# Spectral mixer and squared-ReLU layer on one core: butterfly outputs of three frequency pairs from TensorE, with a reordered first stage

## The chip, the cores and the metric

The kernel runs on 1 core of one Trainium2 chip. The metric is the device time of one execution in microseconds (us). Three runs of the kernel before gave 182.49, 182.58 and 182.77 us, with a median of 182.58 us.

Engine names in the text: PE is TensorE, DVE is VectorE, ACT is ScalarE, POOL is GpSimd, SP is SyncE, which issues most DMAs here. "L333" is line 333 of the kernel before.

## The reference

```python
x = A_x                                   # (1, 2048, 512) bf16
n = layernorm(x)                          # over the last axis
X = rfft2(n) * (w_r + 1j * w_i)           # w: (2048, 257)
h = x + irfft2(X).astype(bfloat16)
t = layernorm(h) @ w1 + b1                # w1: (512, 1792)
h2 = h + (relu(t) ** 2 @ w2 + b2)         # w2: (1792, 512)
```

The two-dimensional transform over 2048 x 512 points is computed as a chain of matrix products with sine and cosine tables that the kernel makes itself.

## The kernel before, in words

The work has three phases, one after the other.

**First phase (statistics and stage 1).** The 2048 rows lie as 16 groups `g` of 128 rows in `xs`. Each group needs a mean and a variance (`mv1`), a reciprocal root (`rs1`), and the table `KF` scaled by it, `KFr[:, g]`, which is called a fold. Means and variances come from DVE (`ln1_stats`, L205 and L208) for 13 groups and from two passes on ACT (`ln1_sums`, L197) for groups 3, 7 and 11. `ln1_rstd` (L211, L212) runs on POOL, `ln1_fold` (L216) on DVE. `stage1(g0)` multiplies groups g0 and g0+1 on PE (L231, L233) and evacuates the result from PSUM into `Bt` with one ACT copy (L241), or, with `split=True`, half on ACT and half on DVE (L238). Beside this, POOL makes the angles of the table GF (`angles_g`, L179), ACT takes their sine (L113), POOL builds the identity `ident`, and POOL issues two gathers (`w_reversed`, L145) that load rows of the weights w in reversed order into `WB`, rows 16 to 22. The spectral step of every pair but the first reads one of these rows.

**Second phase (spectral).** The 16 values of the frequency index k1 are handled as 8 pairs `pr`. For each pair:
- `stage2(pr)`: 8 matmuls of 256 columns (L326), then one ACT copy into `U` (L333); for pair 0 the copy is split (L331).
- `stage3(pr)`: for pairs 1 to 7, 4 matmuls of 512 columns (L351 to L354) give two sums A and B, then one ACT copy puts them into `AB` (L356). Pair 0 is its own case (L343 to L347) and writes `X` directly.
- `butterfly(pr)`: on DVE, A plus swapped B and A minus swapped B give `X` (L365, L366), two instructions.
- `spectral(pr)`: on DVE, two products with the weights (`mA`, `mB`, L375), two instructions into `Z` (L380, L381), two into `M` (L388, L390). The two butterfly instructions of the next pair are placed inside: one before the `Z` pair and one before the `M` pair.
- `stage4(pr)`: 8 matmuls (L405, L406), then one ACT copy into `T` (L413), for the last pair split over ACT and DVE (L410, L411).

The loop over `pr` (L426) issues in each turn `stage3(pr+2)`, `stage2(pr+3)`, `stage4(pr-1)`, `spectral(pr)`. So the ACT queue in a turn reads: copy AB(pr+2), copy U(pr+3), copy T(pr-1). In the turn `pr == 4` the sine of the table GI (L113) follows on ACT behind T(3) and so stands ahead of AB(7). The copies of the transposed tables, `KI` (L418) and `EI` (L258), stand between the other ACT copies. POOL has little to do here: it casts `b1f` (L446).

**Third phase.** Inverse transform over columns (`s5`, `s6`), second layernorm (`norm`, `transp`), and the two matrix products of the layer (L568, L587), in five chunks. Its first matmuls (L471) read `T` of every pair.

Two things set the order of the work. The last call, `pin`, ties each engine to the order in which the program issues its instructions, so an engine never takes a later instruction first. And `mm_tile` gives out PSUM in four buffers of 4 KB for each partition, all of PSUM in the first two phases.

Of the kernel before, what the change touches and what calls it, by code (L numbers as in the profile page):

```python
# [9 lines left out]
ALU = mybir.AluOpType  # L10
ACT = mybir.ActivationFunctionType
FP32 = mybir.dt.float32
BF16 = mybir.dt.bfloat16
I32 = mybir.dt.int32
I16 = mybir.dt.int16
P = 128
# [18 lines left out]
def kernel(  # L35
# [16 lines left out]
    nc = tc.nc  # L52
# [32 lines left out]
    GF = fwd.tile([P, 2, 512], BF16, name="GF")  # L85
    EF = fwd.tile([P, 9, 3, P], BF16, name="EF")
    EI = fwd.tile([P, 9, 3, P], BF16, name="EI")
    KFr = fwd.tile([P, G, 256], BF16, name="KFr")
    Bt = fwd.tile([P, 4, 16, P], BF16, name="Bt")
    mv1 = fwd.tile([P, G, 2], FP32, name="mv1")  # L90
# [20 lines left out]
    def sin_of(dst, fi):  # L111

        nc.scalar.activation(dst, fi.bitcast(I16)[:, ::2], ACT.Sin, scale=SIN_SCALE)  # L113
# [62 lines left out]
    def angles_g(t):  # L176
        o = 512 * t
        for r, q in ((0, QT), (256, HT)):
            nc.gpsimd.tensor_scalar(fiG[:, o + r:o + r + 256], idxL[:, r:r + 256], cols[:, t:t + 1], float(q),  # L179
                                    ALU.mult, ALU.add)  # L180
# [11 lines left out]
    def ln1_sums(g):  # L192

        for f, sc, k in ((ACT.Copy, -float(D) ** -1.5, 0), (ACT.Square, float(D) ** -0.5, 1)):
            junk = fwd.tile([P, D], BF16, tag="junk", bufs=2, name="junk")
            kw = dict(bias=mv1[:, g, 0:1]) if k else {}
            nc.scalar.activation(junk[:], xs[:, g, :], f, scale=sc, accum_out=mv1[:, g, k:k + 1], **kw)  # L197
# [12 lines left out]
    def ln1_rstd(a, b):  # L210
        nc.gpsimd.tensor_scalar(rs1[:, a:b], mv1[:, a:b, 1], EPS, None, ALU.add)  # L211
        nc.gpsimd.tensor_tensor(rs1[:, a:b], rs1[:, a:b], mhalf[:, 0:b - a], ALU.pow)  # L212

    def ln1_fold(a, b, eng=nc.vector):
        for g in range(a, b):
            eng.tensor_scalar(KFr[:, g, :], KF[:], rs1[:, g:g + 1], None, ALU.mult)  # L216

    def stage1(g0, n=0, split=False):
        if split:
            two = [mm_tile("p1a"), mm_tile("p1b")]  # L220
            pts = [pt[:, 0:512] for pt in two]
        else:
            pt = mm_tile("p1")
            pts = [pt[:, 0:512], pt[:, 512:1024]]
        pvs = [o.rearrange("p (e i c) -> p e i c", e=2, i=2) for o in pts]
        warm(pts[0], n)
        for t in range(2):
            for i in range(2):
                g = g0 + i
                o = pvs[t][:, :, i, :]  # L230
                nc.tensor.matmul(o, lhsT=xs[:, g, P * t:P * t + P],  # L231
                                 rhs=KFr[:, g, 0:P].unsqueeze(1).to_broadcast([P, 2, P]), start=True, stop=False)
                nc.tensor.matmul(o, lhsT=xs[:, g, 256 + P * t:256 + P * t + P],  # L233
                                 rhs=KFr[:, g, :].rearrange("p (e c) -> p e c", e=2), start=False, stop=True)
        dst = Bt[:].rearrange("p e q (g s) -> p e g q s", s=8)[:, :, g0:g0 + 2]
        if split:
            for t, cp in ((0, nc.scalar.copy), (1, nc.vector.tensor_copy)):
                cp(dst[:, 2 * t:2 * t + 2], pts[t].rearrange("p (e i q s) -> p e i q s", e=2, i=2, q=16))  # L238
            return two[0][:, 512:1024].bitcast(BF16)
        else:  # L240
            nc.scalar.copy(dst, pt[:].rearrange("p (e i q s) -> p e i q s", e=4, i=2, q=16))  # L241
# [18 lines left out]
    def table_neg(ks):  # L260
        nc.vector.tensor_scalar(EI[:, ks[0]:ks[-1] + 1, 2, :], EI[:, ks[0]:ks[-1] + 1, 0, :], -1.0, None, ALU.mult)

    for g in (3, 7, 11):
        ln1_sums(g)
    ln1_stats(0, 1)
    ln1_rstd(0, 2)
    angles_g(0)
    ln1_stats(2, 4, 5)
    ln1_fold(0, 2)
    stage1(0, 8)  # L270
    ln1_rstd(2, 6)
    angles_g(1)
    ln1_stats(6, 8, 9)
    ln1_fold(2, 6)
    stage1(2)
    ln1_rstd(6, 10)
    stage1(4)
    ln1_stats(10, 12)
    ln1_rstd(10, 12)
    ln1_fold(6, 10)  # L280
    stage1(6)
    ln1_stats(13)
    ln1_fold(10, 12)
    ln1_rstd(12, 14)
    sin_of(GF[:].rearrange("p t c -> p (t c)"), fiG[:])
    stage1(8)
    ln1_stats(14, 15)
    ln1_rstd(14, 16)
    ln1_fold(12, 14)
    stage1(10)  # L290
    nc.gpsimd.memset(ident[:], 0.0)
    nc.gpsimd.affine_select(out=ident[:], in_=ident[:], compare_op=ALU.not_equal,
                            fill=1.0, base=0, pattern=[[-1, P]], channel_multiplier=1)

    nc.vector.tensor_scalar(GF[:, :, 255:256], GF[:, :, 255:256], 0.5, None, ALU.mult)
    ln1_fold(14, 16)
    w_reversed(0)
    w_reversed(1)
    nc.vector.tensor_scalar(EF[:, :, 2, :], EF[:, :, 0, :], -1.0, None, ALU.mult)
    stage1(12, split=True)  # L300
    tr08 = stage1(14, split=True)
    transposed(tr08, (0, 8), True)

    nc.gpsimd.tensor_scalar(cols[:, 4:5], pF[:, 0:1], 256.0, 128.0, ALU.mult, ALU.add)
    nc.gpsimd.tensor_scalar(cols[:, 5:6], pF[:, 0:1], 256.0, 256.0, ALU.mult, ALU.add)
# [29 lines left out]
    def stage3(pr):  # L335
        U = Us.pop(pr)
        if pr == 0:
            Xs[pr] = X = fwd.tile([P, 2, 2, 256], BF16, tag="X", bufs=2, name="X")
            pxs = [mm_tile("p3"), mm_tile("p3b")]
            for u, k1 in ((0, 0), (1, 8)):  # L340
                C, Sp, Sn = EF[:, k1, 1, :], EF[:, k1, 0, :], EF[:, k1, 2, :]
                o = pxs[u][:, 0:512]
                nc.tensor.matmul(o, lhsT=C, rhs=U[:, u, :], start=True, stop=False)  # L343
                nc.tensor.matmul(o[:, 0:256], lhsT=Sp, rhs=U[:, u, 256:512], start=False, stop=False)
                nc.tensor.matmul(o[:, 256:512], lhsT=Sn, rhs=U[:, u, 0:256], start=False, stop=True)
            for u, cp in ((0, nc.scalar.copy), (1, nc.vector.tensor_copy)):
                cp(X[:, u].rearrange("p r c -> p (r c)"), pxs[u][:, 0:512])  # L347
        else:
            px = mm_tile("p3")
            C, Sp, Sn = EF[:, pr, 1, :], EF[:, pr, 0, :], EF[:, pr, 2, :]  # L350
            nc.tensor.matmul(px[:, 0:512], lhsT=C, rhs=U[:, 0, :], start=True, stop=False)  # L351
            nc.tensor.matmul(px[:, 0:512], lhsT=Sn, rhs=U[:, 1, :], start=False, stop=True)
            nc.tensor.matmul(px[:, 512:1024], lhsT=C, rhs=U[:, 1, :], start=True, stop=False)
            nc.tensor.matmul(px[:, 512:1024], lhsT=Sp, rhs=U[:, 0, :], start=False, stop=True)  # L354
            ABs[pr] = AB = fwd.tile([P, 2, 2, 256], BF16, tag="AB", bufs=3, name="AB")
            nc.scalar.copy(AB[:].rearrange("p u r c -> p (u r c)"), px[:])  # L356

    def butterfly(pr):

        AB = ABs[pr]  # L360
        Xs[pr] = X = fwd.tile([P, 2, 2, 256], BF16, tag="X", bufs=2, name="X")
        bsw = AB[:, 1, ::-1, :]

        Xf = X[:].rearrange("p u r c -> p (u r) c")
        return (lambda: nc.vector.tensor_tensor(Xf[:, 0::3], AB[:, 0], bsw, ALU.add),  # L365
                lambda: nc.vector.tensor_tensor(Xf[:, 2:0:-1], AB[:, 0], bsw, ALU.subtract))  # L366

    def spectral(pr):
        X = Xs.pop(pr)
        nxt = butterfly(pr + 1) if pr + 1 < 8 else (lambda: None, lambda: None)  # L370
        mA = fwd.tile([P, 2, 2, 256], BF16, tag="mA", bufs=2, name="mA")
        mB = fwd.tile([P, 2, 2, 256], BF16, tag="mB", bufs=2, name="mB")
        step = 23 - 2 * pr if pr else 8
        for m, w in ((mA, WB[0]), (mB, WB[1])):
            nc.vector.tensor_tensor(m[:], X[:], w[:, pr:pr + step + 1:step, 1:Df].unsqueeze(2).to_broadcast([P, 2, 2, 256]), ALU.mult)  # L375
        Zs[pr] = Z = fwd.tile([P, 2, 2, 256], BF16, tag="Z", bufs=2, name="Z")
        Ms[pr] = M = fwd.tile([P, 2, 2, 256], BF16, tag="M", bufs=2, name="M")
        ABs.pop(pr, None)
        nxt[0]()
        nc.vector.tensor_tensor(Z[:, :, 0], mA[:, :, 0], mB[:, :, 1], ALU.subtract)  # L380
        nc.vector.tensor_tensor(Z[:, :, 1], mA[:, :, 1], mB[:, :, 0], ALU.add)  # L381
        nxt[1]()
        if pr == 0:
            nc.vector.tensor_scalar(M[:, :, 0], Z[:, :, 1], -1.0, None, ALU.mult)
            nc.vector.tensor_copy(M[:, :, 1], Z[:, :, 0])
        else:

            nc.vector.tensor_tensor(M[:, 0], Z[:, 0], Z[:, 1], ALU.add)  # L388
            Zf = Z[:].rearrange("p u r c -> p (u r) c")
            nc.vector.tensor_tensor(M[:, 1], Zf[:, 3::-3], Zf[:, 1:3], ALU.subtract)  # L390
# [24 lines left out]
    stage2(0, split=True)  # L415
    stage2(1)
    stage3(0)
    nc.scalar.copy(KI[:], tr08[:, 4 * P:5 * P])  # L418
    table_i(tr08, (0, 8))
    stage3(1)  # L420
    stage2(2)
    tr = mm_tile("ptr", BF16)
# [240 lines left out]
```

## Time and profile before

| what | value |
|---|---|
| median of three runs | 182.58 us |
| the profiled execution, its own time | 182.58 us |
| its span, first to last instruction | 180.8 us |
| PE busy | 159.7 us (88%), 946 matmuls |
| DVE busy | 122.8 us (68%) |
| ACT busy | 101.1 us (56%) |
| POOL busy | 64.8 us (36%) |
| mean granted PE clock | 0.978 |

The span is what the trace shows between the first and the last instruction; the 1.78 us between span and time lie around it. Busy shares are averages over three phases with different limits, so they say little by themselves: the first phase lasts to about 21.4 us, when stage 2 begins, the second to about 51 us, when DVE finishes `M` of the last pair, and the third to the end. In a timeline line the first number is the start, the second the duration in us; a duration runs past the start of the next instruction on the same engine, because instructions overlap at their ends, so the distance between starts is what one instruction costs its engine. A bracket at the end tells how long the engine idled before and what ended the wait.

### The profile page before, as it was taken

The page shows a single profiled execution, that of the slowest core. Times are in us where ns is not written, and L with a number is a line of the kernel's source. Part 1 is how long each engine was busy: PE and PEld are TensorE (multiplying, and loading weights), DVE is VectorE, ACT ScalarE, POOL GpSimd, SP SyncE. Part 2 cuts the span into 40 slices and gives each one's busy share as a digit, 9 for nine tenths or more (in the row PEclk, how much of TensorE's full clock was granted, in tenths as well). Part 3 has the DMA queues.
Part 4 walks back from the last instruction along what each step waited for, and adds up shares of the span by engine and source line. Part 5 has one row for each costly group of instructions (what it writes and reads, how often), then busy time and mean ns, then how long its engine had stood idle before and what let it go on. Part 6 is the DMA issues. An engine that isn't in the chain of part 4 may idle for free.

```text
span 180.8 us, 2668 instructions
## 1 busy us (share of the span) xinstructions
PE 159.7 (88%) x946; PEld 89.3 (49%) x946; DVE 122.8 (68%) x300; ACT 101.1 (56%) x172; POOL 64.8 (36%) x81
## 2 busy tenths in 40 slices
PE   3479787989978787899998999999999989999991
PEld 1247555756543574365633555444544434556440
DVE  7997579999937387647897248696348794259311
ACT  4987788999624477147923267912267921268200
POOL 5786816999901140205302022512022412025000
PEclk9957999999999999999999999999999999999998
DMA  5999991000000000010000000001010000110010
GB/s 160 319 426 407 353 285 31 0 0 5 0 0 0 2 4 0 2 46 12 4 0 29 29 29 4 0 0 58 29 34 0 0 0 29 58 34 0 0 58 29
DMA packets 7773, 11.19 MB, mean 62 GB/s; under 512 B 2256, under 2 KB 6224, under 8 KB 7504
## 3 DMA queue, kind: packets, MB, share of 16 engines
q1 hardware_dynamic: 7600, 10.11, 16.4%
q0 software_dynamic: 160, 0.92, 1.4%
q8 instruction: 7, 0.11, 0.3%
q14 instruction: 6, 0.05, 0.1%
HBM read 8.93 MB, written 2.10 MB: 61 GB/s over the span
## 4 chain that ended last, share of the span: by engine, by line
PE 55%; DVE 21%; ACT 14%; DMA 3%; issue 3%; POOL 2%; SPq 0%; DVEq 0%; POOLq 0%; ACTq 0%
PE ph L568 22%; PE po L587 21%; DVE act L572 3%; DMA xs<-in_A_x_dram 3%; ACT U L333 3%; PE p L471 3%; DVE hs L486 2%; ACT rl L571 2%; PE p L530 2%; ACT AB L356 2%; DVE st L495 2%; DVE st L205 2%; ACT Bt L241 2%; ACT junk L492 2%; POOL rs L503 1%
## 5 line engine op out<-in xcount | busy, mean ns | idle before, releaser
L568 PE MATMUL ph<-UT,W 128*128 128x384 bf16 (+2 forms) x280 | 53.1, 336 | 0.7 <-ACT UT L534 0.5
L571 ACT ACTIVATE rl<-ph,b1f 128x384 bf16<-128x384 f32 (+2 forms) x70 | 41.2, 603 | 21.0 <-PE ph L568 19.6
L587 PE MATMUL po<-W,act 128*128 128x512 bf16 x224 | 50.8, 379 | 0.0
L572 DVE TENSOR_TENSOR act<-rl 128x384 bf16<-128x384 bf16 (+2 forms) x70 | 32.6, 478 | 17.2 <-ACT rl L571 16.9
L575 POOL TENSOR_TENSOR hb<-hs,b2b 128x512 f32<-128x512 bf16 x16 | 18.5, 1154 | 57.4 <-DVE act L572 55.4
L568 PEld LDWEIGHTS <-W 128*128 128x128 bf16 x280 | 27.4, 98 | 20.7 <-issue 1.4
L587 PEld LDWEIGHTS <-act 128*128 128x128 bf16 x224 | 21.6, 98 | 27.3 <-issue 3.1
L591 DVE TENSOR_TENSOR ot<-po,hb 128x512 bf16<-128x512 f32 x16 | 11.0, 690 | 18.1 <-PE po L587 18.1
L446 POOL CAST b1f<-b1b 128x14 f32<-128x14 bf16 x1 | 20.6, 20559 | 5.3 <-DMA b1b<-in_B_b_dram 5.3
L515 ACT ACTIVATE u<-hs,nm,rs 128x512 bf16<-128x512 bf16 x6 | 4.7, 808 | 25.2 <-DVE nm L512 25.2
L231 PE MATMUL p<-KFr,xs 128*128 128x256 bf16 x24 | 7.8, 348 | 3.5 <-DVE KFr L216 3.5
L486 DVE SCALAR_TENSOR_TENSOR hs<-p,xs 128x512 bf16<-128x512 f32 x16 | 10.8, 679 | 0.1
L471 PE MATMUL p<-GI,T 128*128 128x256 bf16 x64 | 9.4, 272 | 0.4 <-DVE T L411 0.4
L502 POOL TENSOR_SCALAR rs<-mv 128x3 f32<-128x3 f32 (+2 forms) x5 | 1.2, 243 | 22.3 <-DVE mv L496 22.2
L246 PE MATMUL idle<-ones 128*128 128x512 bf16 x37 | 9.0, 379 | 0.0
L485 PE MATMUL p<-R,KI 128*128 128x512 bf16 x16 | 6.1, 381 | 3.2 <-DVE R L481 3.2
L205 DVE BATCH_NORM_STATS2 st<-xs 128x6 f32<-128x512 bf16 x13 | 8.5, 677 | 0.2 <-DMA xs<-in_A_x_dram 0.2
L246 PEld LDWEIGHTS <-ones 128*128 128x128 bf16 x45 | 4.7, 106 | 7.8 <-POOL ones L142 2.9
L326 PE MATMUL p<-GF,Bt 128*128 128x256 bf16 x64 | 8.1, 273 | 0.0
L413 ACT CAST T<-p 128x1024 bf16<-128x1024 f32 x7 | 7.2, 1025 | 1.7 <-PE p L406 1.7
L471 PEld LDWEIGHTS <-T 128*128 128x128 bf16 x64 | 6.2, 98 | 3.5 <-ACT T L410 0.9
L233 PE MATMUL p<-KFr,xs 128*128 128x256 bf16 x24 | 7.9, 351 | 0.0
(134 smaller groups left out, 227.9 us busy)
## 6 DMA issues: line engine op xcount, KB each, us to landing
W<-in_B_w_dram SPq DMA_DIRECT2D x2, 1792.0 KB, 22.3
out_dram<-ot SPq DMA_DIRECT2D x16, 128.0 KB, 1.8
xs<-in_A_x_dram SPq DMA_DIRECT2D x3, 512.0 KB, 6.9
WB<-in_A_w_r_dram SPq DMA_DIRECT2D x1, 1028.0 KB, 9.7
WB<-in_A_w_i_dram SPq DMA_DIRECT2D x1, 1028.0 KB, 11.7
xs<-in_A_x_dram SPq DMA_DIRECT2D x2, 256.0 KB, 3.6
b2b<-in_B_b_dram SPq DMA_DIRECT2D x1, 128.0 KB, 10.5
b1b<-in_B_b_dram SPq DMA_DIRECT2D x1, 3.5 KB, 22.1
```

The lines of the kernel that those rows point to most:

```text
L205: nc.vector.bn_stats(st[:], xs[:, g, :])
L246: nc.tensor.matmul(o, lhsT=ones[:, 0:P], rhs=ones[:], start=True, stop=True)
L326: nc.tensor.matmul(puv[:, :, e, :], lhsT=Bt[:, 2 * t + 1 - e, 2 * pr + q, :], rhs=GFv[:, t, :, e, :], start=(t == 0), stop=(t == 1))
L446: nc.gpsimd.tensor_copy(b1f[:], b1b[:])
L471: nc.tensor.matmul(pe[:, 256 - 256 * e:512 - 256 * e], lhsT=T2[:, lt, g].rearrange("p q s -> p (q s)"), rhs=GI[:, lt, :], start=(r == 0), ...
L486: nc.vector.scalar_tensor_tensor(hs[:, g, :], py[:], WSC, xs[:, g, :], ALU.mult, ALU.add)
L568: nc.tensor.matmul(ph[:, 0:n], lhsT=W1[:, d, bass.ts(f, P)], rhs=UT[:, d, 0:n], start=(d == 0), stop=(d == ND - 1))
L571: nc.scalar.activation(rl[:, 0:n], ph[:, 0:n], ACT.Relu, bias=b1f[:, f:f + 1], scale=1.0)
L572: sq = nc.vector.tensor_tensor(act[:, f, 0:n], rl[:, 0:n], rl[:, 0:n], ALU.mult)
L575: add = nc.gpsimd.tensor_tensor(hb[:, g, :], hs[:, g, :], b2b[:], ALU.add)
L587: nc.tensor.matmul(po[:], lhsT=act[:, f, bass.ts(i, P)], rhs=W2[:, f, :], start=(f == 0), stop=(f == NF - 1))
L591: nc.vector.tensor_tensor(ot[:], po[:], hb[:, g, :], ALU.add)
```

## The change

The diff has three parts.

1. **Butterfly on PE.** For pairs 2, 4 and 6 (`ON_PE`), `stage3` issues 12 matmuls instead of 4: in each half `u`, two of 512 columns and four of 256 columns add up the finished X in PSUM. One ACT copy of the same shape as before writes it to `X`. The two DVE instructions of `butterfly` go for these pairs. `Cn`, the negated cosine of these pairs, is made by one new DVE instruction. `X` has three buffers instead of two.
2. **First phase reordered.** The gathers move from the end of the phase to the front of the POOL queue, one behind the first `ln1_rstd`, one behind the second. `angles_g(0)` and `angles_g(1)` move behind them. The folds of groups 8 and 9 move from DVE to POOL. `ln1_sums(11)` moves behind the evacuation of stage 1's first pair on ACT, the sine of GF ahead of the evacuation of groups 6 and 7, some folds on DVE move, and the evacuation of groups 12 and 13 is one ACT copy and no longer split.
3. **KI and EI.** The copies of `KI` and of `EI` for pair 0 move on ACT from behind `stage3(0)` to ahead of `stage2(0)`.

```diff
+    ON_PE = (2, 4, 6)
+    Cn = fwd.tile([P, len(ON_PE), P], BF16, name="Cn")
...
-    for g in (3, 7, 11):
-        ln1_sums(g)
+    ln1_sums(3)
+    ln1_sums(7)
     ln1_stats(0, 1)
     ln1_rstd(0, 2)
-    angles_g(0)
+    w_reversed(0)
     ln1_stats(2, 4, 5)
     ln1_fold(0, 2)
     stage1(0, 8)
+    ln1_sums(11)
+    angles_g(0)
     ln1_rstd(2, 6)
-    angles_g(1)
+    w_reversed(1)
     ln1_stats(6, 8, 9)
     ln1_fold(2, 6)
     stage1(2)
     ln1_rstd(6, 10)
+    ln1_fold(8, 10, nc.gpsimd)
+    angles_g(1)
     stage1(4)
     ln1_stats(10, 12)
+    ln1_fold(6, 8)
+    sin_of(GF[:].rearrange("p t c -> p (t c)"), fiG[:])
+    stage1(6)
     ln1_rstd(10, 12)
-    ln1_fold(6, 10)
-    stage1(6)
     ln1_stats(13)
-    ln1_fold(10, 12)
     ln1_rstd(12, 14)
-    sin_of(GF[:].rearrange("p t c -> p (t c)"), fiG[:])
     stage1(8)
     ln1_stats(14, 15)
+    ln1_fold(10, 12)
     ln1_rstd(14, 16)
-    ln1_fold(12, 14)
-    stage1(10)
     nc.gpsimd.memset(ident[:], 0.0)
...
+    stage1(10)
+    ln1_fold(12, 14)
+    stage1(12)
+    ln1_fold(14, 16)
+    nc.vector.tensor_scalar(EF[:, :, 2, :], EF[:, :, 0, :], -1.0, None, ALU.mult)
+    nc.vector.tensor_scalar(Cn[:], EF[:, ON_PE[0]:ON_PE[-1] + 1:ON_PE[1] - ON_PE[0], 1, :], -1.0, None, ALU.mult)
 
     nc.vector.tensor_scalar(GF[:, :, 255:256], GF[:, :, 255:256], 0.5, None, ALU.mult)
-    ln1_fold(14, 16)
-    w_reversed(0)
-    w_reversed(1)
-    nc.vector.tensor_scalar(EF[:, :, 2, :], EF[:, :, 0, :], -1.0, None, ALU.mult)
-    stage1(12, split=True)
     tr08 = stage1(14, split=True)
     transposed(tr08, (0, 8), True)
+    nc.scalar.copy(KI[:], tr08[:, 4 * P:5 * P])
+    table_i(tr08, (0, 8))
...
+        elif pr in ON_PE:
+            C, Sp, Sn, Cm = EF[:, pr, 1, :], EF[:, pr, 0, :], EF[:, pr, 2, :], Cn[:, ON_PE.index(pr), :]
+            px = mm_tile("p3")
+
+            for u in range(2):
+                o = px[:, 512 * u:512 * u + 512]
+                nc.tensor.matmul(o, lhsT=C, rhs=U[:, 0, :], start=True, stop=False)
+                nc.tensor.matmul(o, lhsT=Sn, rhs=U[:, 1, :], start=False, stop=False)
+                for r, (ws, wc) in enumerate(((Sp, C), (Sn, Cm)) if u == 0 else ((Sn, Cm), (Sp, C))):
+                    other = slice(256 - 256 * r, 512 - 256 * r)
+                    orr = o[:, 256 * r:256 * r + 256]
+                    nc.tensor.matmul(orr, lhsT=ws, rhs=U[:, 0, other], start=False, stop=False)
+                    nc.tensor.matmul(orr, lhsT=wc, rhs=U[:, 1, other], start=False, stop=(r == 1))
+            Xs[pr] = X = fwd.tile([P, 2, 2, 256], BF16, tag="X", bufs=3, name="X")
+            nc.scalar.copy(X[:].rearrange("p u r c -> p (u r c)"), px[:])
...
-        nxt = butterfly(pr + 1) if pr + 1 < 8 else (lambda: None, lambda: None)
+        nxt = butterfly(pr + 1) if pr + 1 < 8 and pr + 1 not in ON_PE else (lambda: None, lambda: None)
...
     stage3(0)
-    nc.scalar.copy(KI[:], tr08[:, 4 * P:5 * P])
-    table_i(tr08, (0, 8))
     stage3(1)
```

More of the change, by code (lines that the diff above doesn't have):

```diff
@@ L337, in stage3 @@
         if pr == 0:
-            Xs[pr] = X = fwd.tile([P, 2, 2, 256], BF16, tag="X", bufs=2, name="X")
+            Xs[pr] = X = fwd.tile([P, 2, 2, 256], BF16, tag="X", bufs=3, name="X")
             pxs = [mm_tile("p3"), mm_tile("p3b")]
@@ L347, in stage3 @@
                 cp(X[:, u].rearrange("p r c -> p (r c)"), pxs[u][:, 0:512])
+        elif pr in ON_PE:
[10 more added lines that the diff above has]
+                    nc.tensor.matmul(orr, lhsT=wc, rhs=U[:, 1, other], start=False, stop=(r == 1))
+            Xs[pr] = X = fwd.tile([P, 2, 2, 256], BF16, tag="X", bufs=3, name="X")
+            nc.scalar.copy(X[:].rearrange("p u r c -> p (u r c)"), px[:])
         else:
@@ L360, in butterfly @@
         AB = ABs[pr]
-        Xs[pr] = X = fwd.tile([P, 2, 2, 256], BF16, tag="X", bufs=2, name="X")
+        Xs[pr] = X = fwd.tile([P, 2, 2, 256], BF16, tag="X", bufs=3, name="X")
         bsw = AB[:, 1, ::-1, :]
```

## The prediction, as it was put on record

> **What bounds the kernel now.** I read the chain of waits first. Its last stretch of the spectral phase is DVE alone from 37.65 us to 50.93 us, and then it goes over to PE (stage 4 of pair 7), ACT and everything behind. So whatever moves DVE's last `M` moves the end of the kernel by as much. The busy time by stretches says the same; its columns after the sum are PE, weight loads, DVE, ACT, POOL and the granted PE clock:
>
> ```profile
> 34.60:37.70 3.10, 2.79 (x23) 1.96 (x22) 3.10 (x9) 2.84 (x3) 3.10 (x1) 1.00 0.00 0
> 37.70:40.80 3.10, 2.79 (x23) 1.97 (x21) 3.10 (x9) 2.84 (x3) 3.10 (x1) 1.00 0.00 0
> ```
>
> DVE is full, 3.10 of 3.10 us. But PE and ACT are close behind (2.79 and 2.84), so the next question is what they wait for. The waits of PE between 24 and 50 us have one row: L351, the first matmul of stage 3, waited 7 times for ACT's copy of U. The timelines of ACT and PE show one turn:
>
> ```profile
> 36.62 0.38 PE L351 MATMUL p<-U,EF 128*128 128x512 bf16 x1 [0.31 <-ACT U L333]
> ...
> 37.26 0.38 PE L354 MATMUL p<-U,EF 128*128 128x512 bf16 x1
> ```
>
> ```profile
> 37.72 1.01 ACT L356 CAST AB<-p 128x1024 bf16<-128x1024 f32 x1 [0.24 <-ACT T L413]
> 38.63 1.02 ACT L333 CAST U<-p 128x1024 bf16<-128x1024 f32 x1
> 39.53 1.03 ACT L413 CAST T<-p 128x1024 bf16<-128x1024 f32 x1
> 40.80 1.01 ACT L356 CAST AB<-p 128x1024 bf16<-128x1024 f32 x1 [0.24 <-ACT T L413]
> ```
>
> This is a closed ring. Stage 3 starts at 36.62; ACT copies AB at 37.72 (1.10 later, as soon as the last matmul is out of PE); the copy of U follows in ACT's fixed order 0.91 later; the next stage 3 starts 1.07 after that, at 39.70. Together 3.08 us a turn. DVE needs 3.22 (mA at 38.31, the next mA at 41.53). So **the ring runs at 3.08 right behind a DVE at 3.22**; DVE is the bound by 0.14 us a turn only. At pair 7 the lead of the ring is small:
>
> ```profile
> 44.48 1.02 ACT L356 CAST AB<-p 128x1024 bf16<-128x1024 f32 x1
> ```
>
> ```profile
> 45.96 0.42 DVE L365 TENSOR_TENSOR X<-AB 128x512 bf16<-128x512 bf16 x1
> ...
> 47.98 0.69 DVE L375 TENSOR_TENSOR mA<-X,WB 128x1024 bf16<-128x1024 bf16 x1
> 48.58 0.69 DVE L375 TENSOR_TENSOR mB<-X,WB 128x1024 bf16<-128x1024 bf16 x1
> 49.30 0.43 DVE L380 TENSOR_TENSOR Z<-mA,mB 128x512 bf16<-128x512 bf16 x1
> 49.64 0.42 DVE L381 TENSOR_TENSOR Z<-mA,mB 128x512 bf16<-128x512 bf16 x1
> 50.17 0.43 DVE L388 TENSOR_TENSOR M<-Z 128x512 bf16<-128x512 bf16 x1
> 50.51 0.42 DVE L390 TENSOR_TENSOR M<-Z 128x512 bf16<-128x512 bf16 x1
> ```
>
> AB(7) is there at 45.50, and its butterfly at 45.96 needs 0.04 of handing over (AB(1): done 26.46, read 26.50). Slack: 0.42 us.
>
> **Part 1, the butterfly.** *What DVE saves.* Two instructions of 0.335 us (start to start) go, three times: 2.01 us. But the last turn above has no butterfly inside already, and it shows what that costs: Z starts 0.72 after mB instead of 0.60, M 0.53 after Z instead of 0.34, because each now waits for the result just before it. That turn takes 47.98 to 50.51 plus 0.34, 2.87 us, against 3.22. So the saving is 0.35 a turn, 1.05 us in all, and not 2.01.
>
> *What the ring pays.* Four matmuls of 512 columns start 0.215 apart (36.62 to 37.26 for three steps). A 256-column matmul that adds to a sum costs 0.109 (the rows of pair 0, L344 and L345). The new stage 3 is two halves of 2 x 0.215 + 4 x 0.109 = 0.866, so its last matmul starts 1.62 after its first; that one lasts 0.27, and the handing over adds 0.08: ACT can copy at 1.97 instead of 1.10. The ring pays 0.87 in each of three turns, **2.61 us**, for the copy into X has the shape of the copy into AB (1.01 us) and stands in its place: U of the next pair is behind it on ACT, and the next stage 3 behind that. Stage 2 and stage 4 behind the longer stage 3 on PE fit: 1.73 + 0.87 + 0.87 is 3.47 of a turn of 3.95.
>
> *The sum.* AB(7) moves from 44.48 to 47.09; ahead of it T(3) and the sine of GI move along, still in its way. Its slack takes 0.42: the butterfly of pair 7 starts **2.19 us later**, and from there DVE does what it did. On the way DVE waits for AB(3) 0.73, for AB(5) 0.96 and for AB(7) 1.55, together 3.24, which eats its 1.05 and gives 2.19. If the 256-column matmuls went at the pace of their weight loads (0.098 a row), the ring would pay 0.26 less. If the sine of GI (0.96, of which 0.6 delays AB(7)) found a gap, 0.6 less.
>
> By the Trainium skill, Perfetto Trace Analysis, Identifying the Most-Contended Engine, one improves the engine with the highest occupancy; that is DVE in this stretch, and by that rule the three butterflies would be worth up to their 2.01 us, a time of 180.6. The ACT and PE rows above speak against it.
>
> `Cn` is one more instruction like the 0.29 us of L261, on a DVE that idles 0.92 before 20.73: nothing. The third X buffer: nothing, since no copy waited for one; if DVE's delay holds X longer, the buffer covers it.
>
> **Part 2, the first phase.** It ends when stage 2 starts (21.37). In its last 5 us ACT never idles. Up to there I follow POOL, whose queue is what changes: reciprocal roots of groups 0, 1 end at 7.09; gather 1.45 (its rows: 1.23 and 0.94, with 0.2 to 0.3 idle ahead); `angles_g(0)` 1.0; roots of 2 to 5 1.43 (8.51 to 9.94). They are out at 11.0 instead of 9.94. DVE waits for them about 0.3 (it was free at 10.71), and stage 1 of groups 2, 3 starts at 11.44 instead of 11.10. PE's granted clock is 0.50 there, so each pair takes 1.7 us as before; ACT copies groups 4, 5 at 15.05 instead of 14.71. Then it has the sine of GF (0.96) and four full copies (0.91) up to the last half copy: 15.05 + 0.91 + 0.96 + 3.64 = 20.56 instead of 20.42. So **+0.15**.
>
> The rest of POOL's queue: second gather 1.35, roots 1.48, folds of 8 and 9, `angles_g(1)` 1.0 (at 15.9, the sine of GF wants it at 15.97), three more roots of 1.05 to 1.1. The last root comes at 19.1 instead of 17.60, its half copy on DVE at 20.65, against 20.73: just in time. No fold on POOL is in the trace. Its nearest row is L179 on POOL, same width and one input, 0.48; below lies DVE's own 0.28, above the two-input L575 with 1.15. I take 0.48, 0.96 for two. At 1.15 the queue is 1.34 later, and nearly all of it reaches the end; at best the gathers are 0.3 shorter. So this part lies between -0.2 and +1.4.
>
> Where the gathers go early nothing is won: the second landed 8.4 us after its issue at 19.86, at 28.3, and pair 1 reads it at 29.05. They push W1 and W2 back by 0.92 MB, which are first read at 61.23. `ln1_sums(11)` (1.46) moves into a time in which ACT waits for PE (0.85 before 13.00).
>
> A row bears on the fold: POOL's cast of 14 numbers took 20.56 us while DVE ran instructions with two inputs, and ended at 49.32, in DVE's first pause.
>
> ```profile
> 28.76 20.56 POOL L446 CAST b1f<-b1b 128x14 f32<-128x14 bf16 x1 [5.28 <-DMA b1b<-in_B_b_dram]
> ```
>
> The Trainium skill, SBUF — State Buffer, Who interferes with whom, explains such rows: the two engines share a port pair that one holds for a whole instruction, and a scaling on VectorE can take it too. By it the folds of 8, 9 on POOL and of 6, 7 on DVE, released by the same roots, exclude each other: about 0.5 us more, 185.4.
>
> **Part 3, KI and EI.** ACT idles 1.0 before 22.02; the two copies cost 0.66 there, after the transposes end at about 21.5. They push the half copy of U(0) by 0.2, and L343 reads it only at 23.13. Where they stood nothing is won: AB(1) at 25.45 waits for L354, done at 25.42. Without that cover, 0.2.
>
> **Sum.** The span was 180.8 and the run 182.58, which is the median too; 1.78 lies around the span. 180.8 + 2.19 + 0.15 + 1.78 = **184.9 us**.
>
> **The rivals.**
> - *POOL's queue ends last in the first phase* (slower, more): folds at 1.15. Then 184.9 + 1.25 = **186.1**. For it: angles, roots and folds in one queue, with 0.1 us to spare. Against: POOL's rows beside a busy DVE there keep their length. 9%.
> - *DVE stays the bound* (faster). Were the ring no ring, so that U of the next pair did not wait behind the copy into X, DVE would keep its 1.05: 182.58 - 1.05 = **181.5**. It decides from the point at which a longer stage 3 costs less than 0.42 us over three turns, 0.14 each, against 0.87 worked out; and with AB(7) where it was, no more than 0.42 could be won. Against it stand the seven waits of L351 and ACT's pinned order. 9%.
> - *Both cancel* within 0.2%: half of the ring's price hidden and the first phase gaining. 4%.
>
> That the change does not do what it says I exclude: the order of each queue is pinned.
>
> **Numbers.** The forecast's case has 78%. Its own ends: 184.9 - 0.26 - 0.6 - 0.35 (first phase at -0.2) = 183.7, a little below for the sizes, and 186.2 with the first phase at +1.4. The range 183.5 to 186.2 leaves out the 13% of the other two cases and a little. A measurement of this kernel tells 0.2% from no change, 0.37 us. Faster 0.09, same 0.04, slower 0.87.
>
> **What would show it.** After: copies into X about 1.97 after their stage 3 starts, and AB and X copies 3.1 and 3.95 us apart in turn; DVE idle ahead of L365 for pairs 3, 5 and 7, released by ACT's AB, about 0.7, 1.0, 1.5; DVE's last M near 53; stage 2 starting near 21.5. Wrong: DVE without waits there, or stage 3 of pairs 2, 4, 6 not delaying the next copy of U.

## The result, and the profile after

The changed kernel takes **185.76 us** (median of 4 runs, 185.75 to 185.78) against 182.54 us for the kernel before beside it. The ratio is 1.018, with a 95% interval of 1.016 to 1.020: slower, as forecast, by 3.2 us where 2.3 were forecast.

The profiled execution has a span of 184.0 us against 180.8. Three points in the two traces divide the 3.2 us:

| stretch | before | after | difference |
|---|---|---|---|
| first phase, up to the start of stage 2 | 21.37 | 22.45 | +1.08 |
| second phase, from there to the end of DVE's last M | 29.48 | 31.60 | +2.12 |
| third phase, from there to the end | 129.95 | 129.95 | 0 |

(The end of the last M is its start plus 0.34.) The third phase is as long as before; it is only pushed.

**The second phase.** First the timelines of PE and ACT of the changed kernel; the instructions here are L361 to L367 (stage 3 of pair 4), L369 (the copy into X), L340 (U), L435 (T) and L378 (AB):

```profile
35.47 0.38 PE L361 MATMUL p<-U,EF 128*128 128x512 bf16 x1 [0.26 <-ACT U L340]
...
37.10 0.27 PE L367 MATMUL p<-U,EF 128*128 128x256 bf16 x1
...
39.43 0.38 PE L373 MATMUL p<-U,EF 128*128 128x512 bf16 x1 [0.31 <-ACT U L340]
```

```profile
37.45 1.01 ACT L369 CAST X<-p 128x1024 bf16<-128x1024 f32 x1 [1.11 <-issue]
38.36 1.02 ACT L340 CAST U<-p 128x1024 bf16<-128x1024 f32 x1
39.26 1.03 ACT L435 CAST T<-p 128x1024 bf16<-128x1024 f32 x1
40.49 1.01 ACT L378 CAST AB<-p 128x1024 bf16<-128x1024 f32 x1 [0.20 <-PE p L376]
...
44.41 1.01 ACT L369 CAST X<-p 128x1024 bf16<-128x1024 f32 x1 [1.07 <-PE p L367]
```

Stage 3 of pair 4 starts at 35.47 and ACT's copy into X only at 37.45, 1.98 later instead of 1.10. ACT stands idle for 1.11 us ahead of it. The bracket there names no releaser (`issue`); the same copy for pair 6, at 44.41, is released by the last matmul of its stage 3 (L367), and 37.45 lies behind the last matmul of pair 4 in the same way. U of pair 5 follows at 38.36, and stage 3 of pair 5 waits for that copy. The turn takes 3.96 us; the next one, of an ordinary pair, 3.05 (39.43 to 42.48).

Then the waits of DVE between 4 and 53 us (who waited for whom, total us, times, longest):

```profile
DVE KFr L218 <- POOL rs L214: 3.2, 5, 1.3
DVE X L387 <- ACT AB L378: 1.6, 3, 1.0
...
DVE EI L263 <- ACT EI L260: 0.9, 1, 0.9
DVE M L410 <- PE p L428: 0.8, 2, 0.5
```

DVE was full in this phase before; now it waits 1.6 for AB (0.21 of it is the wait for AB(1), which the kernel before had too), 0.9 for EI and 0.8 for a buffer of M. The last wait decides, that of the butterfly of pair 7:

```profile
49.16 0.43 DVE L387 TENSOR_TENSOR X<-AB 128x512 bf16<-128x512 bf16 x1 [1.03 <-ACT AB L378]
```

It started at 45.96 before; 3.20 later, of which 1.08 come from the first phase.

**The first phase.** The first row of DVE's waits is new as well: 3.2 us for reciprocal roots from POOL. The timelines of POOL and ACT show why:

```profile
12.74 1.05 POOL L214 TENSOR_TENSOR rs<-rs,mhalf 128x4 f32<-128x4 f32 x1
13.89 1.93 POOL L218 TENSOR_SCALAR KFr<-KF,rs 128x256 bf16<-128x256 bf16 x2
15.91 0.94 POOL L181 TENSOR_SCALAR fiG<-idxL,cols 128x256 int32<-128x256 int32 x2
```

```profile
16.89 1.06 ACT L115 ACTIVATE GF<-fiG 128x1024 bf16<-128x1024 int16 x1 [1.24 <-POOL fiG L181]
17.85 3.77 ACT L243 CAST Bt<-p 128x1024 bf16<-128x1024 f32 x4
```

The two folds on POOL take 1.93 us. The angles of GF come behind them, so ACT idles 1.24 and starts the sine of GF at 16.89; four copies of stage 1 stand behind that one in ACT's order.

### The profile page after: what moved, and what is told of

Its sections match the earlier page's. It is cut to its first block, busy times and chain, and to the rows that moved or that the text cites. A ratio compares the mean times of both kernels' runs of the same rounds, so it can differ in the third digit from the quotient of the medians.

```text
span 184.0 us, 2708 instructions
## 1 busy us (share of the span) xinstructions
PE 161.3 (88%) x970; PEld 90.8 (49%) x970; DVE 121.7 (66%) x292; ACT 101.7 (55%) x172; POOL 46.4 (25%) x83
## 4 chain that ended last, share of the span: by engine, by line
PE 53%; ACT 17%; DVE 15%; POOL 6%; issue 3%; DMA 3%; SPq 0%; POOLq 0%; DVEq 0%; ACTq 0%
PE ph L588 21%; PE po L607 20%; ACT U L340 4%; DVE act L592 3%; DMA xs<-in_A_x_dram 3%; PE p L491 3%; DVE hs L506 2%; ACT rl L591 2%; ACT AB L378 2%; ACT Bt L243 2%; PE p L550 2%; DVE st L515 2%; ACT junk L512 1%; POOL rs L523 1%; ACT X L369 1%
## 5 line engine op out<-in xcount | busy, mean ns | idle before, releaser
L233 PE MATMUL p<-KFr,xs 128*128 128x256 bf16 x28 | 7.6, 305 | 5.8 <-DVE KFr L218 5.5
L520 POOL TENSOR_TENSOR nm<-mv 128x1 f32<-128x1 f32 x5 | 1.4, 289 | 32.7 <-ACT junk L512 32.7
L435 ACT CAST T<-p 128x1024 bf16<-128x1024 f32 x7 | 7.1, 1020 | 1.2 <-PE p L428 1.2
L554 ACT COPY UT<-p 128x768 bf16<-128x768 bf16 (+2 forms) x5 | 4.2, 842 | 6.5 <-PE p L550 6.5
L515 DVE BATCH_NORM_STATS2 st<-hs 128x6 f32<-128x512 bf16 x11 | 7.6, 689 | 0.2
```

The costliest lines, as they stand in the source:

```text
L515: nc.vector.bn_stats(st[:], hs[:, g, :])
```

## The experiments

The length of the first phase changes from run to run. Two things in it differ between the profiles: the time at which `xs` arrives (DVE's wait for it ends at 6.77 in the kernel before and at 7.62 in fold_on_dve), and the stretch in which the matmuls of stage 1 go at half pace, 0.21 us from start to start instead of 0.11 (it lasts until about 15.8 in the kernel before and about 13.9 in the changed one). The length of the second phase, read from each profile like above, hardly varies: 29.48 and 29.57 us in two kernels that share it, 31.60, 31.61, 31.59 and 31.60 in four others. So it is the finer measure of part 1, and stands beside the times. Each phase length comes from one profile. The rows were not all measured on one chip, so a time is to be compared with the kernel before that ran beside it.

| run | median us | kernel before, beside it | ratio, 95% interval | stage 2 starts | second phase |
|---|---|---|---|---|---|
| before | 182.54 | | | 21.37 | 29.48 |
| after | 185.76 | 182.54 | 1.018 (1.016 to 1.020) | 22.45 | 31.60 |
| butterfly_alone | 184.90 | 182.76 | 1.0113 (1.0070 to 1.0157) | 21.57 | 31.61 |
| first_phase_alone | 183.69 | 182.76 | 1.0066 (1.0041 to 1.0092) | 22.44 | 29.57 |
| fold_on_dve | 185.00 | 182.76 | 1.0140 (1.0105 to 1.0174) | 22.04 | 31.59 |
| ring_cut | 182.01 | 182.76 | 0.9970 (0.9948 to 0.9993) | 21.08 | 28.85 |
| ring_cut_dve | 183.37 | 182.83 | 1.0033 (1.0010 to 1.0057) | 20.79 | 29.81 |
| one_pair | 182.54 | 182.83 | 0.9999 (0.9967 to 1.0030) | 20.67 | 29.90 |
| gi_later | 185.14 | 182.83 | 1.0144 (1.0106 to 1.0181) | 22.52 | 30.95 |
| gathers_late | 185.04 | 182.83 | 1.0131 (1.0097 to 1.0165) | 21.77 | 31.60 |
| ring_cut_ident | 182.10 | 182.24 | 0.9999 (0.9976 to 1.0022) | 21.15 | 28.85 |
| ring_cut_ei | 182.65 | 182.24 | 1.0030 (0.9999 to 1.0061) | 21.73 | 28.93 |

The theory is that of the prediction: a ring of stage 3, its copy on ACT and the copy of the next U sets the second phase, and POOL's queue the first. The rivals are named in each expectation.

### The two parts, each alone

butterfly_alone is the kernel before with `ON_PE`, `Cn`, the new branch of `stage3` and the third buffer of `X`. first_phase_alone is the changed kernel with

```diff
-    ON_PE = (2, 4, 6)
+    ON_PE = ()
```

> Part 1 alone: pairs 2, 4 and 6 get their butterfly from TensorE, the first phase and the KI and EI copies are those of the kernel before. Ring theory: the copies of U wait behind the later copies into X, 2.61 us less a slack of 0.42, so 2.1 to 2.2 us slower than before, near 184.7. Rival, DVE stays the bound: 1.05 us faster, near 181.5. Rival, the second phase cost little and the first phase all of it: near 182.5.

> Parts 2 and 3 alone: no pair has its butterfly on TensorE, the first phase is the reordered one. If the two parts add up, 1.08 us slower than before (stage 2 starts at 22.45 in place of 21.37), near 183.6. If the late start of stage 2 were swallowed by a wait further on, near 182.5.

Measured: +2.14 us and +0.93 us. They add up to 3.07, against 3.2 for the whole change. In the second phase butterfly_alone pays 2.13, and first_phase_alone 0.09; in the first phase it is the other way round (+0.20, within what that phase varies by, and +1.07). So the parts add up, within what the first phase varies by, and with three pairs on PE DVE did not stay the bound.

### How much each pair costs

```diff
-    ON_PE = (2, 4, 6)
+    ON_PE = (6,)
```

on top of butterfly_alone (the slice for `Cn` is cut to pair 6).

> Part 1 alone, and of the pairs only 6 on TensorE, in the old order of the turn. Ring theory, a charge of 0.87 us a pair behind a slack of 0.42: the second phase is 0.45 us longer than before, 29.9 in place of 29.5. Rival, every pair costs the same third of the 2.13 us that three cost: 0.71 longer, 30.2. Rival, DVE the bound: 0.35 shorter.

The second phase takes 29.90, 0.42 more than before: the charge of one pair less the slack, and not a third of what three pairs cost (0.71). DVE finishes the turn without a butterfly early and then waits for AB(7):

```profile
45.67 0.43 DVE L383 TENSOR_TENSOR X<-AB 128x512 bf16<-128x512 bf16 x1 [0.68 <-ACT AB L374]
```

One pair on PE already wins nothing. The time (182.54) cannot tell 0.4 us here: its interval is 0.997 to 1.003, and in the profiled run the first phase was 0.70 shorter than before (20.67).

### The ring cut

```diff
+    stage2(3)
     stage3(2)
     for pr in range(9):
+        if 0 < pr and pr + 3 < 8:
+            stage2(pr + 3)
         if 0 < pr and pr + 2 < 8:
             stage3(pr + 2)
-        if pr + 3 < 8:
-            stage2(pr + 3)
```

ring_cut is butterfly_alone with this order: the same instructions, but on PE and ACT the work on U of the next pair goes ahead of stage 3 and its copy. ring_cut_dve is the kernel before, all butterflies on DVE, with this order alone.

> Part 1 alone with the order of each turn changed: stage 2 of pair n+1 and its copy of U go ahead of stage 3 of pair n and its copy, on PE and on ACT. The work is the same. Ring theory: no copy of U waits behind a copy into X any more, DVE is the bound again and keeps its 1.05 us, so near 181.5. Rival, PE's or ACT's added work itself is too much (PE 3.03 us a turn on average, ACT 2.84, DVE 3.05): near 184.7, as without the new order.

> The kernel before, all butterflies on DVE, with the new order of the turn only (stage 2 and its copy ahead of stage 3 and its copy). Ring theory: the ring at 3.08 us was behind DVE at 3.22 anyway, so cutting it alone wins nothing: from the start of stage 2 to the end of DVE's last M 29.5 us as before, the time that of the kernel before. Rival, the new order is a gain by itself and the pairs on TensorE have no part in it: a second phase of about 28.9 us, as in the run with both.

ring_cut is 2.9 us under butterfly_alone, and its second phase 2.76 shorter (28.85 against 31.61) with the same work on every engine. That rules out the rival that PE or ACT simply have too much to do. The timeline of ACT in ring_cut (L336 is U, L365 X, L431 T, L374 AB) has no idle time ahead of X for pair 4:

```profile
33.60 1.07 ACT L336 CAST U<-p 128x1024 bf16<-128x1024 f32 x1
34.76 1.01 ACT L365 CAST X<-p 128x1024 bf16<-128x1024 f32 x1
35.67 1.02 ACT L431 CAST T<-p 128x1024 bf16<-128x1024 f32 x1
36.57 1.03 ACT L336 CAST U<-p 128x1024 bf16<-128x1024 f32 x1
37.48 1.04 ACT L374 CAST AB<-p 128x1024 bf16<-128x1024 f32 x1
```

It is also under the kernel before, by 0.63 us in the second phase where 1.05 were expected. The missing 0.42 are about the size of two waits that DVE now meets, 0.21 for AB(3) (the butterfly starts 0.81 after mB, at 32.87, instead of 0.60) and 0.21 for the second gather:

```profile
29.05 0.69 DVE L393 TENSOR_TENSOR mB<-X,WB 128x1024 bf16<-128x1024 bf16 x1 [0.21 <-DMA WB<-in_A_w_i_dram,idxR]
```

ring_cut_dve shows that the order wins nothing by itself: its second phase is 29.81, 0.33 longer than before. Nearly all of that is a new wait for AB(2), whose copy now stands behind that of U(3): the butterfly starts 0.91 after mB (28.47) instead of 0.60.

```profile
29.38 0.45 DVE L365 TENSOR_TENSOR X<-AB 128x512 bf16<-128x512 bf16 x1 [0.21 <-ACT AB L356]
```

So what ring_cut wins comes from the pairs on TensorE, and only when the ring is cut.

### The sine of GI in the way

```diff
-        if pr == 4:
+        if pr == 6:
             sin_of(GI[:].rearrange("p t c -> p (t c)"), fiI[:])
```

(The cast of b1f moves with it.)

> The changed kernel with the sine of GI two turns later, behind T(5) in place of T(3), so that it no longer stands ahead of the copy AB(7) on ACT. Ring theory: AB(7) starts as soon as its matmuls are out of PE, about 47.5 in place of 48.12, and the time falls by about 0.6 us, to 185.15. If the butterfly of pair 7 waits for something else, nothing changes: 185.76.

185.14 us where 185.15 was expected, a second phase 0.65 shorter than in the changed kernel (30.95 against 31.60), and AB(7) at 47.53 behind its matmuls and not behind ACT's own queue:

```profile
46.32 1.02 ACT L435 CAST T<-p 128x1024 bf16<-128x1024 f32 x1
47.53 1.01 ACT L378 CAST AB<-p 128x1024 bf16<-128x1024 f32 x1 [0.20 <-PE p L376]
```

So of the 2.12 us about 1.5 remain when AB(7) need not wait for the sine of GI, and 0.65 go with that wait. The kernel before had the same sine ahead of AB(7), where it took from a slack and cost nothing; it costs time only once the ring has eaten the slack.

### POOL's queue

fold_on_dve takes the two folds off POOL, gathers_late the two gathers:

```diff
-    ln1_fold(8, 10, nc.gpsimd)
...
-    ln1_fold(6, 8)
+    ln1_fold(6, 10)
```

```diff
-    w_reversed(0)
...
-    w_reversed(1)
...
                             fill=1.0, base=0, pattern=[[-1, P]], channel_multiplier=1)
+    w_reversed(0)
+    w_reversed(1)
```

> The changed kernel with the folds of groups 8 and 9 back on DVE. Theory: POOL's two folds took 1.93 us of its queue in place of 0.96 and all behind them was late; without them the angles of GF are ready 1.9 us earlier, ACT then sets the pace again, stage 2 starts at about 21.2, and the time is 1.2 us less than the changed kernel's, near 184.5. Rival, the gathers at the front of the queue are what delays the phase: the time stays near 185.5.

> The changed kernel with both gathers back behind the identity on POOL's queue, the folds of groups 8 and 9 still on POOL. If POOL's queue as a whole sets the end of the first phase, taking 2.7 us of gathers out of it is worth as much as taking the folds out of it: stage 2 starts at 21.3 or so in place of 22.45 and the time is 184.7. If only the folds on POOL matter: 185.7.

Both win, 0.76 and 0.72 us, less than the 1.2 and 1.1 expected. Neither is the sole cause: each shortens the queue, and when it is short enough something else comes last. In both profiles the sine of GF no longer waits for the angles from POOL, as it did for 1.24 us in the changed kernel; it follows a copy of stage 1 that waited for PE. These lines are from gathers_late:

```profile
15.29 1.01 ACT L243 CAST Bt<-p 128x1024 bf16<-128x1024 f32 x1 [0.69 <-PE p L235]
16.20 1.06 ACT L115 ACTIVATE GF<-fiG 128x1024 bf16<-128x1024 int16 x1
```

In the profiled run of fold_on_dve the data was late too: DVE waited for `xs` until 7.62, against 6.78 in the changed kernel, and stage 1 began at 9.69 instead of 8.60.

```profile
7.62 0.69 DVE L207 BATCH_NORM_STATS2 st<-xs 128x6 f32<-128x512 bf16 x1 [1.08 <-DMA xs<-in_A_x_dram]
```

Its runs range from 184.58 to 185.47; the lower end is near the 184.5 expected. How much of the 1.08 belongs to folds and how much to gathers these runs do not say; a queue has no such shares.

### Two tries at more

```diff
+    w_reversed(0)
+    w_reversed(1)
     nc.gpsimd.memset(ident[:], 0.0)
```

in ring_cut, instead of behind the identity (ring_cut_ident); and on top of that the tables of pairs 4 to 7 later (ring_cut_ei):

```diff
-        if pr == 0:
+        if pr == 2:
             transposed(tr, (4, 5, 6, 7))
             table_i(tr, (4, 5, 6, 7))
-        if pr == 1:
+        if pr == 3:
             table_neg((4, 7))
```

> As the run with part 1 and the new order of the turn, and on POOL's queue the two gathers ahead of the two instructions that make the identity (0.5 us). There DVE's mB of pair 1 waited 0.21 us for the second gather. With that wait gone the second phase is 0.2 us shorter, 28.6 to 28.7, and the time about 1.0 us under the kernel before. If the identity comes late for the transposes, stage 2 starts later instead.

> As the run with the gathers ahead of the identity, and the transposes of the tables for pairs 4 to 7, with their copy on ACT and their negation on DVE, two turns later. That copy stood on ACT ahead of U(4) and AB(3), and DVE waited about 0.2 us for AB(3). Without it a second phase of 28.4 to 28.5 us; if the copy pushes a later AB instead, no gain over the run beside it.

Neither won. In ring_cut_ident the wait for the gather is gone and the second phase is 28.85 as before: DVE arrives 0.2 earlier at the butterfly of pair 3 and waits longer there.

```profile
32.93 0.43 DVE L383 TENSOR_TENSOR X<-AB 128x512 bf16<-128x512 bf16 x1 [0.33 <-ACT AB L374]
```

In ring_cut_ei that wait is gone, and the same 0.33 stands ahead of the butterfly of pair 5 (28.93). The copy of EI, which had stood ahead of U(4) and AB(3), now stands on ACT ahead of U(6) and AB(5), at 36.78. And in this order there is little left to win in a turn: in ring_cut, between 34.90 and 40.97, PE is busy for all of 6.07 us, DVE for 5.93 and ACT for 5.57. ring_cut stays the best version, 0.997 of the kernel before. That gain in time is small: ring_cut_ident has the same second phase and came out level with the kernel before beside it (0.9976 to 1.0022). The 0.63 us of the second phase are the firmer evidence.

## Why the prediction was right, point by point

The time lies in the stated range and the second phase went as worked out. The first phase did not: there the first of the rivals came true in kind, to which the prediction gave 9%. POOL's queue did end last, and the measured 185.76 is nearer to that rival's 186.1 than to the forecast's 184.9. The range held because its upper end had been drawn with the slow folds in it.

- **The ring, right in mechanism and size.** A longer stage 3 was priced at 0.87 us a pair; it took 0.88 for pair 4 (1.98 instead of 1.10), and the turn 3.96 against 3.95. Three pairs and the slack gave 2.19; the second phase grew by 2.12. ring_cut, which moves only the order, shows the ring as the cause, and one_pair the slack.
- **What DVE saves, right.** 0.35 a turn and not 0.67, because the butterfly had filled the pauses between dependent instructions. In ring_cut the turn of pair 3, in which DVE does not wait and makes no butterfly, goes from 34.89 to 37.75, 2.86 us (2.87 predicted).
- **DVE's waits, right in sum and wrong in place.** Forecast were 3.24 us ahead of AB(3), AB(5) and AB(7). They came to 3.20, but 0.92 stood ahead of the negation of EI, whose copy had been pushed behind X(2) on ACT, and 0.84 ahead of two M, whose buffers stage 4 on the delayed PE had not yet read. Neither was in the prediction; both lay inside time that DVE would otherwise have spent waiting for AB, since AB(5) and AB(7) came at the time the ring set.
- **The first phase, mis-sized.** This is the step that failed: "I take 0.48, 0.96 for two", for the folds on POOL. They took 1.93, 0.97 each, nearer to the upper row with 1.15. The row of 0.48 has the same width and one input but works on int32, and the fold on bf16; whether the type makes the difference no run tried alone. Most of what stood around it held: the roots of groups 2 to 5 were out at 11.04 (11.0 predicted), stage 1 of groups 2, 3 began at 11.41 (11.44), the last half copy on ACT at 21.52, 0.96 after the 20.56 predicted, which is the 0.97 by which the folds were longer. One thing did not: ACT copied groups 4 and 5 at 14.64 and not at 15.05, because stage 1 left its half pace sooner than in the kernel before. It did not show in the time, since ACT then waited for POOL until 16.89. With 1.93 in the sum the forecast would have been 185.9.
- **The rule on the shared port, not borne out here as priced.** By the Trainium skill, SBUF — State Buffer, Who interferes with whom, the folds of both engines could exclude each other; the prediction put 0.5 us more on it. Released by the same roots, DVE's two (from 13.82) took 0.70 us instead of 0.47 beside POOL's 1.93 (from 13.89). In gathers_late DVE's began 0.33 after POOL's and took 0.45, and POOL's were again 1.93. So POOL's time looks like its own pace and not a wait for DVE's folds; POOL's folds with DVE at rest are in no run.
- **The rule on the most-contended engine, misleading here.** The Trainium skill, Perfetto Trace Analysis, Identifying the Most-Contended Engine, points at DVE. It had the highest occupancy, and taking work off it made the kernel slower, because the engine that took it over stood in a ring only 0.14 us a turn behind. In ring_cut the same offload shortens the second phase by 0.63 us.
- **KI and EI, right as far as seen.** The second phase of first_phase_alone, which has these copies in their new place, is 0.09 from that of before; no run moved them alone.

## What to carry to other kernels

Before work is moved off the fullest engine, follow the waits of the engine that is to take it: a copy that stands in a fixed order ahead of the next stage's input closes a ring, and the ring pays the whole of the new work, while the full engine saves only what its own pauses leave. Often the order is the cheaper edit; here the same instructions with two blocks swapped went from 1.1% slower to 0.3% faster. And on an engine with a full queue, each added instruction delays all behind it: where no row of the same engine, width and data type gives its price, carry the dearer row in the sum as well.

## What the runs showed of the hardware that was not expected

- Where POOL's queue set the end of the first phase, the run times hardly vary: 183.63 to 183.72 in eight runs of first_phase_alone, 185.75 to 185.78 in four of the changed kernel. The kernel before ranges from 181.52 to 183.88 beside these experiments. In the profiled runs, the matmuls that go at half pace (0.21 from start to start instead of 0.11) end at 13.71 in the changed kernel and at 14.35 in first_phase_alone, and stage 2 starts at 22.45 and 22.44: what varies is hidden behind POOL. In gi_later stage 1 began 0.76 later than in the changed kernel (9.36 against 8.60), and stage 2 only 0.07 (22.52).
- POOL's cast of `b1f`, 14 numbers in each partition, took 20.56 us in the kernel before and 0.20 in the changed one:

```profile
28.86 0.20 POOL L466 CAST b1f<-b1b 128x14 f32<-128x14 bf16 x1 [5.31 <-DMA b1b<-in_B_b_dram]
```

It began 0.10 us later in the run. In the kernel before DVE went without a pause until 49.3, and the cast ended at 49.32; in the changed kernel it fell beside a scaling with one tensor input that DVE began at 28.91. But a scaling on DVE at 31.66 did not let it through in the kernel before. The other runs point to DVE's pauses: in one_pair the cast took 12.78 us and ended at 42.18, just after the first Z that had to wait for its mB, in the first turn without a butterfly:

```profile
29.40 12.78 POOL L464 CAST b1f<-b1b 128x14 f32<-128x14 bf16 x1 [5.62 <-DMA b1b<-in_B_b_dram]
```

```profile
42.15 0.42 DVE L398 TENSOR_TENSOR Z<-mA,mB 128x512 bf16<-128x512 bf16 x1
```

In six more runs it took 0.36 to 1.21 us and ended 0.02 to 0.03 after the start of such a Z or M. first_phase_alone does not fit (0.54 us, ended at 29.69 without such a pause), so the rule stays open, and nothing here tried it alone. It costs nothing, since `b1f` is read after 60 us.
